# First taps on ScalarE, one parked group, another group order and wider blocks in a convolution plus MLP kernel

## The chip, the cores and the metric

The kernel runs on one core of one Trainium2 chip. The metric is the device time of one execution in microseconds (us); where several executions were timed, the median is given. PE is TensorE, PEld its weight loads, DVE VectorE, ACT ScalarE, POOL GpSimd, SP the engine that issues most DMAs.

## The reference

```python
# x: (8, 4224, 192) f32, weight: (8 heads, 7 taps), w_ch1: (192, 768), w_ch2: (768, 192)
w = softmax(weight, axis=-1)                       # per head
x_pad = six zero rows ahead of each sequence
a[b, s, h, :] = sum_k w[h, k] * x_pad[b, s + k, h, :]     # causal convolution, 24 channels a head
xn = (a - mean(a)) / sqrt(var(a) + 1e-6) * g_ln           # over the 192 channels
out = a + relu(xn @ w_ch1) @ w_ch2
```

## The kernel before

Each of the 128 partitions holds 33 consecutive rows of a sequence. A sequence is worked off in groups of n rows a partition: 16 and 17 for seven sequences, and four smaller groups for the first one, so that TensorE can start early. The mean is folded into the first weights and the factor 1/std is applied at the end, so `up` needs only the transposed convolution. PSUM is the memory that the matmuls write; here it is used as eight banks. To move a finished bank out, so that it can be written again, is called its eviction: ScalarE does it for `up` (L371), VectorE for `down` (L394).

```python
for n in (6, 8, 10, R - 24) if b == 0 else (J - 1, J):   # R = 33, J = 17: 6, 8, 10, 9, then 16, 17
...
xpool: bufs=2   ypool: bufs=3   hid ("ht"): bufs=1   psum: 8 banks of 512 f32, one tag, taken in turn
...
def first_tap(g):                # y = tap 0 * x, one instruction a head (n x 24 elements)
    ...                          # groups 0 and 1 on ACT (L284), all others on DVE (L286)
def conv(g):                     # y += tap k * x shifted by k: 6 taps x 8 heads on DVE (L294)
def transpose(g): ...            # DVE, 32 x 32 blocks (L302)
def stats(g): ...                # DVE: bn_stats a row (L315), then a short chain to 1/std

def up(g):                       # first matmul, four 32-row tiles at a time, into four banks
    half = n if n <= 11 else (n + 1) // 2
    for f in range(NF):                                   # 6 slices of 128 hidden units
        for i0 in range(0, n, half):                      # blocks of rows
            ph = [psum.tile([P, 512], F32, tag="ps", ...) for q in range(NQ)]
            for c in range(NC):                           # 6 channel chunks
                for q in range(NQ):                       # one "round": four matmuls, w columns
                    nc.tensor.matmul(ph[q][:, 0:w], w1[rows, c, fs], t[rows, js, c, :], ...)   # L366
            for q in range(NQ):
                nc.scalar.activation(ht[g][:, f, js, q, :], ph[q]..., AF.Relu)                # L371

def down(g):                     # second matmul, two rows to a bank
    for i0 in range(0, n, 2):
        po = psum.tile([P, 512], F32, tag="ps", ...)
        ... six matmuls a row into po (L389) ...
        for j, dst in zip(js, at):
            nc.vector.scalar_tensor_tensor(out=yg[:, j, :], in0=dst, scalar=rstd..., in1=yg[:, j, :],
                                           op0=ALU.mult, op1=ALU.add)                         # L394
        ... output DMA when a group is done ...

first_tap(0); conv(0); centre_w1(); keep_warm(24); first_tap(1); transpose(0); ... prepare w2 ...
for g in range(NG):
    if g + 2 < NG: load_x(g + 2)
    if g == 0: conv(1)
    up(g)
    if g + 1 < NG:
        if g > 0: first_tap(g + 1); conv(g + 1)
        transpose(g + 1)
    stats(g)
    down(g)
```

Each engine works off its own instructions in program order, and waits by semaphores for data, for a PSUM bank or for a buffer. The float32 matmuls count as two instructions each in the trace.

Of the kernel before, what the change touches and what calls it, by code (L numbers as in the profile page):

```python
# [7 lines left out]
F32 = mybir.dt.float32  # L8
# [3 lines left out]
ALU = mybir.AluOpType  # L12
# [4 lines left out]
def kernel(  # L17
# [23 lines left out]
    nc = tc.nc  # L41
    PSUM = bass.MemoryType.PSUM
    B, S, D = x.shape
    H, K = weight.shape
    F = moe_w_ch1.shape[1]
    P = 128
    Q = 64
    C = 32
    GRP = D // H
    PAD = K - 1  # L50
    R = S // P
    J = 17
    NF = F // P
# [7 lines left out]
    groups = []  # L61
    for b in range(B):
        j0 = 0
        for n in (6, 8, 10, R - 24) if b == 0 else (J - 1, J):
            groups.append((b, j0, n))
            j0 += n
        assert j0 == R
    assert max(n for _, _, n in groups) <= J
    NG = len(groups)
# [4 lines left out]
    outr = out.rearrange("b (p r) d -> b p (r d)", p=P)  # L74

    consts = ctx.enter_context(tc.tile_pool(name="consts", bufs=1))
    setup = ctx.enter_context(tc.tile_pool(name="setup", bufs=1))
# [5 lines left out]
    psum = ctx.enter_context(tc.tile_pool(name="ps", bufs=8, space=PSUM))  # L83
# [54 lines left out]
    for r in range(2):  # L138
        nc.scalar.dma_start(out=gb[Q * r : Q * r + Q, :], in_=g_col[P:D, :])
    nc.sync.dma_start(  # L140
        out=taps, in_=bass.AP(tensor=weight.tensor, offset=0, ap=[[0, P], [K, H], [1, K]])
    )
    nc.sync.dma_start(
        out=raw1[:, 0:2].rearrange("p s f w -> p (s f w)"), in_=w1_words[0:P, :]
    )
    for r in range(2):
        nc.sync.dma_start(
            out=raw1[Q * r : Q * r + Q, 2, :, :].rearrange("p f w -> p (f w)"),
            in_=w1_words[P:D, 2 * FH * r : 2 * FH * (r + 1)],
# [3 lines left out]
        out=raw2.rearrange("p (c d) w -> p c (d w)", d=D),  # L153
        in_=w2_words.rearrange("(c p) d -> p c d", p=P),
# [78 lines left out]
    for q in range(NQ):  # L233
        m = copy[C * q : C * q + C].rearrange("p (q i) -> p q i", q=NQ)
        nc.gpsimd.affine_select(
            out=m, in_=m, pattern=[[0, NQ], [-1, C]],
# [37 lines left out]

    y, yt, rstd = {}, {}, {}

    def first_tap(g):
        n = groups[g][2]
        y[g] = ypool.tile([P, J, D], F32, tag="y", name=f"y{g}")
        for h in range(H):  # L280
            cs = slice(h * GRP, h * GRP + GRP)
            dst, src, tap = y[g][:, 0:n, cs], xg[g][:, 0:n, cs], taps[:, h, 0:1]
            if g < 2:
                nc.scalar.mul(dst, src, tap)  # L284
            else:
                nc.vector.tensor_scalar(out=dst, in0=src, scalar1=tap, scalar2=None, op0=ALU.mult)  # L286

    def conv(g):
        n = groups[g][2]
        t = xg.pop(g)  # L290
        for k in range(1, K):
            for h in range(H):
                cs = slice(h * GRP, h * GRP + GRP)
                nc.vector.scalar_tensor_tensor(  # L294
                    out=y[g][:, 0:n, cs], in0=t[:, k : k + n, cs], scalar=taps[:, h, k : k + 1],
                    in1=y[g][:, 0:n, cs], op0=ALU.mult, op1=ALU.add,
                )

    def transpose(g):
        n = groups[g][2]  # L300
        yt[g] = tpool.tile([P, J, NC, C], F32, tag="yt", name=f"yt{g}")
        nc.vector.transpose(  # L302
            yt[g][:, 0:n].rearrange("p j c t -> p (j c t)"),
            y[g][:, 0:n].rearrange("p j d -> p (j d)"),
        )

    def stats(g):
        n = groups[g][2]
        st = spool.tile([P, J, nc.vector.BN_STATS_DIM], F32, tag="st", name=f"st{g}")
        dt = spool.tile([P, J], F32, tag="d", name=f"d{g}")  # L310
        vt = spool.tile([P, J], F32, tag="v", name=f"v{g}")
        rt = spool.tile([P, J], F32, tag="r", name=f"r{g}")
        d, v, r = dt[:, 0:n], vt[:, 0:n], rt[:, 0:n]
        for j in range(n):
            nc.vector.bn_stats(out=st[:, j, :], in_=y[g][:, j, :])  # L315


        nc.vector.tensor_tensor(d, st[:, 0:n, 1], st[:, 0:n, 4], op=ALU.subtract)
        nc.vector.tensor_tensor(v, st[:, 0:n, 2], st[:, 0:n, 5], op=ALU.add)
        nc.vector.scalar_tensor_tensor(  # L320
            out=d, in0=d, scalar=0.25, in1=d, op0=ALU.mult, op1=ALU.mult
        )
        nc.vector.scalar_tensor_tensor(
            out=v, in0=v, scalar=1.0 / D, in1=d, op0=ALU.mult, op1=ALU.add
        )
        nc.vector.tensor_scalar(v, v, scalar1=1e-6, scalar2=None, op0=ALU.add)


        nc.vector.tensor_single_scalar(
            d.bitcast(U32), v.bitcast(U32), 1, op=ALU.logical_shift_right  # L330
        )
        nc.vector.tensor_scalar(
            out=r.bitcast(I32), in0=d.bitcast(I32), scalar1=-1.0, scalar2=float(0x5F3759DF),
            op0=ALU.mult, op1=ALU.add,
        )
        for _ in range(3):
            nc.vector.tensor_tensor(d, r, r, op=ALU.mult)  # L337
            nc.vector.scalar_tensor_tensor(  # L338
                out=d, in0=d, scalar=-0.5, in1=v, op0=ALU.mult, op1=ALU.mult
            )  # L340
            nc.vector.scalar_tensor_tensor(  # L341
                out=r, in0=d, scalar=1.5, in1=r, op0=ALU.add, op1=ALU.mult
            )
        rstd[g] = rt
# [3 lines left out]
    def up(g):  # L348
        n = groups[g][2]
        t = yt.pop(g)  # L350
        ht[g] = hpool.tile([P, NF, J, NQ, C], F32, tag="ht", name=f"ht{g}")

        half = n if n <= 11 else (n + 1) // 2
        for f in range(NF):
            fs = slice(f * P, f * P + P)
            for i0 in range(0, n, half):
                js = slice(i0, min(i0 + half, n))
                w = (js.stop - js.start) * C
                ph = [
                    psum.tile([P, 512], F32, tag="ps", name=f"ph{g}_{f}_{i0}_{q}")  # L360
                    for q in range(NQ)
                ]
                for c in range(NC):
                    for q in range(NQ):
                        rows = slice(C * q, C * q + C)
                        nc.tensor.matmul(  # L366
                            ph[q][:, 0:w], w1[rows, c, fs], t[rows, js, c, :],
                            start=(c == 0), stop=(c == NC - 1),
                        )
                for q in range(NQ):  # L370
                    nc.scalar.activation(  # L371
                        ht[g][:, f, js, q, :],
                        ph[q][:, 0:w].rearrange("p (j t) -> p j t", t=C), AF.Relu,
                    )

    def down(g):
        b, j0, n = groups[g]
        t = ht.pop(g)
        yg = y.pop(g)

        ends = (n,) if g + 1 < NG else (4, 8, 12, 14, 16, n)
        done = 0
        for i0 in range(0, n, 2):
            js = range(i0, min(i0 + 2, n))
            po = psum.tile([P, 512], F32, tag="ps", name=f"po{g}_{i0}")
            at = [po[:, i * D : i * D + D] for i in range(len(js))]
            for j, dst in zip(js, at):
                for f in range(NF):
                    nc.tensor.matmul(  # L389
                        dst, t[:, f, j, :, :].rearrange("p q t -> p (q t)"), w2[:, f, :],  # L390
                        start=(f == 0), stop=(f == NF - 1),
                    )
            for j, dst in zip(js, at):
                nc.vector.scalar_tensor_tensor(  # L394
                    out=yg[:, j, :], in0=dst, scalar=rstd[g][:, j : j + 1],
                    in1=yg[:, j, :], op0=ALU.mult, op1=ALU.add,
                )
            if js[-1] + 1 in ends:
                end = js[-1] + 1
                nc.sync.dma_start(  # L400
                    out=outr[b, :, (j0 + done) * D : (j0 + end) * D],
                    in_=yg[:, done:end].rearrange("p j d -> p (j d)"),
                )
                done = end


    first_tap(0)
    conv(0)
    centre_w1()
    keep_warm(24)  # L410
    first_tap(1)
    transpose(0)
    words_2 = (
# [4 lines left out]
    for g in range(NG):  # L418
        if g + 2 < NG:
            load_x(g + 2)  # L420
        if g == 0:
            conv(1)
        up(g)
        if g + 1 < NG:
            if g > 0:
                first_tap(g + 1)
                conv(g + 1)
            transpose(g + 1)
        stats(g)
        down(g)  # L430


# [28 lines left out]
```

## Time and profile before

| | before |
|---|---|
| median | 1080.33 us (1079.67 to 1080.75, 5 runs) |
| span of the profiled execution | 1078.5 us |
| busy: PE, DVE, ACT | 98%, 70%, 24% |
| mean granted TensorE clock | 0.997 |

Three groups of instructions, from the list of groups by shape (line, engine, operation, out<-in, shapes, count | busy us, mean ns of one | idle time just before them and what ended it):

```profile
L366 PE MATMUL ph<-yt,w 32*128 32x256 f32 x6336 | 357.7, 377 | 4.3 <-DVE y L394 4.3
L371 ACT ACTIVATE ht<-ph 128x256 f32<-128x256 f32 x528 | 160.0, 390 | 418.3 <-PE ph L366 418.3
L394 DVE SCALAR_TENSOR_TENSOR y<-po,r,y 128x192 f32<-128x192 f32 x264 | 96.8, 412 | 306.2 <-PE po L389 304.3
```

ACT and DVE wait hundreds of microseconds for PE, which costs nothing: PE is the bound. The one figure that costs is the small one, 4.3 us in which PE waited for L394.

### The profile page before, as it was taken

Reading aid. Unit: us, or ns where it says so; the run is one execution under the profiler, and the core shown is the slowest. Engines: PE = TensorE matmul, PEld = TensorE weight load, DVE = VectorE, ACT = ScalarE, POOL = GpSimd, SP = SyncE. Lnnn points to the kernel's source line nnn. Section 1 sums busy time; section 2 is a strip of 40 time slices with the busy share of each in tenths; the row PEclk is TensorE's granted clock in tenths of the full one; section 3 lists DMA queues with packets and bytes.
Section 4 is the critical chain, followed back from the end, with each engine's and each line's share of the span. In section 5 each row is a group of like instructions: output and inputs, shape, how many; then the busy total and the mean of one; then the engine's idle time right before and its main releaser. Section 6 shows DMA issues by size and latency. Waiting matters only on the chain.

```text
span 1078.5 us, 27860 instructions
## 1 busy us (share of the span) xinstructions
PE 1057.6 (98%) x12488; PEld 997.0 (92%) x12488; DVE 753.5 (70%) x1851; ACT 255.4 (24%) x806; POOL 11.1 (1%) x23
## 2 busy tenths in 40 slices
PE   4999999999999999999999999999999999999998
PEld 3988998998999999999999989999899999999998
DVE  7999699849397692957749396693947849297301
ACT  5322122214031230403204041130402214031230
POOL 1000000000000000000000000000000000000000
PEclk9999999999999999999999999999999999999999
DMA  5122123030030300303021030301203030010101
GB/s 184 60 79 111 38 86 115 2 111 35 1 144 1 144 2 16 129 2 144 1 96 50 1 145 1 144 2 51 94 1 144 2 123 23 1 64 1 60 2 63
DMA packets 7718, 66.69 MB, mean 62 GB/s; under 512 B 1199, under 2 KB 2351, under 8 KB 3758
## 3 DMA queue, kind: packets, MB, share of 16 engines
q1 hardware_dynamic: 7294, 64.91, 15.8%
q8 instruction: 97, 1.59, 0.6%
q14 instruction: 23, 0.19, 0.1%
q10 hardware_dynamic: 304, 0.00, 0.0%
HBM read 38.95 MB, written 25.95 MB: 60 GB/s over the span
## 4 chain that ended last, share of the span: by engine, by line
PE 91%; DVE 8%; DMA 1%; issue 0%; ACT 0%; SPq 0%; DVEq 0%
PE ph L366 45%; PE po L389 45%; DVE y L294 5%; DVE yt L302 1%; DMA room<-in_moe_w_ch_dram 1%; DVE st L315 0%; DVE y L286 0%; DVE y L394 0%; ACT room L174 0%; DVE room L182 0%; DVE power L182 0%; DVE w L188 0%; ACT power L174 0%; DVE d L338 0%; DVE r L341 0%
## 5 line engine op out<-in xcount | busy, mean ns | idle before, releaser
L366 PE MATMUL ph<-yt,w 32*128 32x256 f32 (+3 forms) x9216 | 524.0, 383 | 4.3 <-DVE y L394 4.3
L366 PEld LDWEIGHTS ph<-yt,w 32*128 32x128 f32 x9216 | 471.6, 186 | 53.3 <-DVE y L394 5.8
L389 PEld LDWEIGHTS po<-w,ht 128*128 128x128 f32 x3168 | 514.3, 190 | 6.0 <-issue 6.0
L389 PE MATMUL po<-w,ht 128*128 128x192 f32 x3168 | 519.6, 327 | 0.0
L294 DVE SCALAR_TENSOR_TENSOR y<-xg,taps,y 128x384 f32<-128x384 f32 (+5 forms) x864 | 429.8, 578 | 0.0
L371 ACT ACTIVATE ht<-ph 128x256 f32<-128x256 f32 (+3 forms) x768 | 237.8, 396 | 772.3 <-PE ph L366 772.3
L394 DVE SCALAR_TENSOR_TENSOR y<-po,r,y 128x192 f32<-128x192 f32 x264 | 96.8, 412 | 306.2 <-PE po L389 304.3
L315 DVE BATCH_NORM_STATS2 st<-y 128x6 f32<-128x192 f32 x264 | 69.7, 341 | 0.0
L302 DVE STREAM_TRANSPOSE yt<-y 128x3072 f32<-128x3072 f32 (+5 forms) x18 | 56.0, 3112 | 0.6
L286 DVE TENSOR_SCALAR y<-xg,taps 128x408 f32<-128x408 f32 (+3 forms) x128 | 43.1, 410 | 0.0
L106 POOL MEMSET xg<- 1x1152 f32 x7 | 7.3, 1047 | 819.2 <-DMA xg<-in_x_dram 432.2
L244 PE MATMUL pm<-room 128*128 128x384 f32 x4 | 3.1, 880 | 12.3 <-DVE room L190 12.3
L244 PEld LDWEIGHTS pm<-room 128*128 128x128 f32 x4 | 1.2, 324 | 12.9 <-issue 12.9
L337 DVE TENSOR_TENSOR d<-r 128x16 f32<-128x16 f32 (+5 forms) x54 | 9.4, 175 | 1.9
L341 DVE SCALAR_TENSOR_TENSOR r<-d,r 128x16 f32<-128x16 f32 (+5 forms) x54 | 9.4, 175 | 1.9
L338 DVE SCALAR_TENSOR_TENSOR d<-d,v 128x16 f32<-128x16 f32 (+5 forms) x54 | 9.4, 174 | 1.9
L272 PEld LDWEIGHTS idle<-room 128*128 128x128 f32 x48 | 5.4, 192 | 0.5 <-ACT w L266 0.5
L272 PE MATMUL idle<-room 128*128 128x128 f32 x48 | 5.6, 277 | 0.0
L284 ACT ACTIVATE y<-xg,taps 128x144 f32<-128x144 f32 (+1 forms) x16 | 5.5, 473 | 0.0
L266 ACT COPY w<-pw 128x384 f32<-128x384 f32 x12 | 4.7, 546 | 1.4 <-PE pw L261 1.4
L245 PE MATMUL pm<-room 128*128 128x384 f32 x4 | 3.1, 880 | 1.2 <-DVE room L190 1.2
L245 PEld LDWEIGHTS pm<-room 128*128 128x128 f32 x4 | 1.2, 324 | 2.9 <-issue 2.9
(48 smaller groups left out, 59.5 us busy)
## 6 DMA issues: line engine op xcount, KB each, us to landing
xg<-in_x_dram SPq DMA_DIRECT2D x7, 2208.0 KB, 12.3
xg<-in_x_dram SPq DMA_DIRECT2D x7, 2112.0 KB, 11.7
out_dram<-y SPq DMA_DIRECT2D x7, 1536.0 KB, 6.0
out_dram<-y SPq DMA_DIRECT2D x6, 1632.0 KB, 6.5
xg<-in_x_dram SPq DMA_DIRECT2D x1, 1536.0 KB, 6.3
xg<-in_x_dram SPq DMA_DIRECT2D x1, 1440.0 KB, 7.6
xg<-in_x_dram SPq DMA_DIRECT2D x1, 1344.0 KB, 10.6
raw<-in_moe_w_ch_dram SPq DMA_DIRECT2D x1, 1152.0 KB, 7.9
```

What stands on the lines that cost most here:

```text
L272: nc.tensor.matmul(idle[:, 0:P], less, copy, start=True, stop=True)
L286: nc.vector.tensor_scalar(out=dst, in0=src, scalar1=tap, scalar2=None, op0=ALU.mult)
L294: nc.vector.scalar_tensor_tensor(out=y[g][:, 0:n, cs], in0=t[:, k : k + n, cs], scalar=taps[:, h, k : k + 1], in1=y[g][:, 0:n, cs], op0=AL ...
L302: nc.vector.transpose(yt[g][:, 0:n].rearrange("p j c t -> p (j c t)"), y[g][:, 0:n].rearrange("p j d -> p (j d)"),)
L315: nc.vector.bn_stats(out=st[:, j, :], in_=y[g][:, j, :])
L337: nc.vector.tensor_tensor(d, r, r, op=ALU.mult)
L338: nc.vector.scalar_tensor_tensor(out=d, in0=d, scalar=-0.5, in1=v, op0=ALU.mult, op1=ALU.mult)
L341: nc.vector.scalar_tensor_tensor(out=r, in0=d, scalar=1.5, in1=r, op0=ALU.add, op1=ALU.mult)
L366: nc.tensor.matmul(ph[q][:, 0:w], w1[rows, c, fs], t[rows, js, c, :], start=(c == 0), stop=(c == NC - 1),)
L371: nc.scalar.activation(ht[g][:, f, js, q, :], ph[q][:, 0:w].rearrange("p (j t) -> p j t", t=C), AF.Relu,)
L389: nc.tensor.matmul(dst, t[:, f, j, :, :].rearrange("p q t -> p (q t)"), w2[:, f, :], start=(f == 0), stop=(f == NF - 1),)
L394: nc.vector.scalar_tensor_tensor(out=yg[:, j, :], in0=dst, scalar=rstd[g][:, j : j + 1], in1=yg[:, j, :], op0=ALU.mult, op1=ALU.add,)
```

## The change

Its intent is to let PE run without a gap after setup. ScalarE copies ("parks") group 0's second matmul into SBUF, so that group 1 gets its banks without VectorE. First taps go to ScalarE while `down` runs, except group 3's, whose y buffer is still group 0's. The third and fourth group swap sizes. Blocks of `up` are 512 columns wide in groups of 16 rows, but for the last slice.

```diff
-        for n in (6, 8, 10, R - 24) if b == 0 else (J - 1, J):
+        for n in (6, 8, 9, R - 23) if b == 0 else (J - 1, J):
...
-    def first_tap(g):
+    def first_tap(g, on_act=True):
...
-            if g < 2:
+            if on_act:
                 nc.scalar.mul(dst, src, tap)
...
-        half = n if n <= 11 else (n + 1) // 2
         for f in range(NF):
+            half = n if n <= 11 or n * C <= 512 and f < NF - 1 else (n + 1) // 2
...
     # down(g) keeps its matmuls; the VectorE step and the output DMA move to finish(g)
+    def park(g):
+        parked = setup.tile([P, n, D], F32, name=f"parked{g}")
+        for i0 in range(0, n, 2):
+            for j in range(i0, min(i0 + 2, n)):
+                nc.scalar.copy(parked[:, j, :], po[g][j])
+                po[g][j] = parked[:, j, :]
...
     for g in range(NG):
         if g + 2 < NG:
             load_x(g + 2)
-        if g == 0:
-            conv(1)
         up(g)
         if g + 1 < NG:
-            if g > 0:
-                first_tap(g + 1)
-                conv(g + 1)
+            conv(g + 1)
             transpose(g + 1)
-        stats(g)
+        if g != 1:
+            stats(g)
         down(g)
+        if g == 0:
+            park(0)
+        elif g == 1:
+            stats(1)
+            finish(0)
+            finish(1)
+        else:
+            finish(g)
+        if g + 2 < NG:
+            first_tap(g + 2, on_act=g != 1)
```

## The prediction

> **What bounds the kernel now.** I read the page's busy shares first. TensorE is busy for 98% of the span, VectorE 70%, ScalarE 24%, so only time in which TensorE stands still or runs slowly is to be had. Then I read the chain of work that ended last, in order of time (start, length, what):
>
> ```profile
> 53.56 1.55 DVE st L315 x6
> ...
> 58.24 0.75 DVE y L394 x2
> 59.00 0.04 issue
> 59.04 16.20 PE ph L366 x238
> 75.24 15.80 PE po L389 x96
> 91.04 19.59 PE ph L366 x288
> ...
> 168.07 0.32 DVE y L394
> ...
> 168.87 33.03 PE ph L366 x570
> 201.90 31.40 PE po L389 x192
> 233.29 33.21 PE ph L366 x576
> ...
> 1042.00 33.36 PE po L389 x204
> 1075.37 0.03 issue
> 1075.39 0.42 DVE y L394
> ```
>
> L366 is the first matmul, `up`; L389 the second, `down`; L394 the VectorE step that scales a `down` result and adds it to y, and so frees its PSUM bank. From 201.90 to 1075 the chain is TensorE alone. It leaves TensorE only before 30 us (setup), at 53 to 59 us and at 130 to 169 us. At 59 us, group 1's `up` needs a bank in which group 0's `down` result still lies; VectorE was busy with conv(1) until 51.76, then transpose and statistics. At 168 us, group 4's `up` waits in the same way for group 3's result, behind first tap and conv of a group of 16.
>
> The stretches tell what the two places cost: the two disturbed `up` phases of groups 1 and 4, then clean ones of 17 and of 16 rows (columns: bounds, length, busy time by engine, granted TensorE clock, DMA):
>
> ```profile
> 53.98:75.24 21.26, 19.49 (x290) 16.89 (x289) 20.67 (x70) 6.44 (x22) 0.00 (x0) 0.92 0.28 100
> 165.65:201.90 36.25, 33.77 (x578) 31.10 (x577) 35.73 (x78) 13.72 (x46) 1.05 (x1) 0.95 0.23 86
> 233.29:266.50 33.21, 33.21 (x578) 29.42 (x577) 33.13 (x64) 13.97 (x44) 0.00 (x0) 1.00 0.31 118
> 299.85:331.14 31.29, 31.29 (x578) 29.42 (x577) 31.21 (x58) 13.34 (x44) 1.05 (x1) 1.00 0.33 125
> ```
>
> A clean `up` of 16 rows takes 31.29 us; group 4's took 36.25, so 4.96 are lost. Group 1 has 8 rows: half of (31.29 - 0.21) plus 0.21 for the phase's start (worked out below) is 15.75; it took 21.26, so 5.51 are lost. Together 10.5 us, though the list of waits puts only 4.3 us of TensorE idle down to L394. The rest is the last column but two: the clock. In the shorter stretches after each wait it is halved:
>
> ```profile
> 60.00:62.00 2.00, 2.00 (x25) 1.50 (x27) 2.00 (x9) 0.00 (x0) 0.00 (x0) 0.76 0.44 182
> 62.00:64.00 2.00, 2.00 (x24) 1.78 (x20) 2.00 (x7) 0.00 (x0) 0.00 (x0) 0.50 1.05 297
> 64.00:66.00 2.00, 2.00 (x36) 1.85 (x36) 2.00 (x6) 1.21 (x4) 0.00 (x0) 0.88 1.01 403
> ...
> 171.00:173.00 2.00, 2.00 (x24) 1.73 (x23) 2.00 (x7) 0.74 (x3) 0.00 (x0) 0.50 0.54 221
> ```
>
> That is 0.08 x 21.26 + 0.05 x 36.25 = 3.5 us of clock; the other 7 us is waiting, part of it bank by bank.
>
> **What the Trainium skill says.** "TensorE: Matmul & The Clock Gate", Part 1: the clock is gated to half after an idle window of about 3.4 us and released after a busy one. The trace agrees: 0.50 after each wait. The same page, "Back-to-back issue gap": a warm matmul costs N/2.4 + 2.5 ns. The trace agrees: a `down` phase of 17 rows takes 33.35 us and one of 16 takes 31.40, so 12 instructions of 192 columns take 1.95 us, 162.5 ns each = 2 x 192/2.4 + 2.5 (an fp32 matmul is two instructions, each two cycles a column). "ScalarE: Activation LUTs", "What ACT_TABLE_LOAD costs": 186 ns + 0.833 ns an element, about 93 more for a pointer operand, 93 overlapped. The trace agrees: eight first taps of 192 elements take 2.96 us, 347 ns apart by the formula. "PSUM — Partial Sum Buffer", on bank collisions: engines must be kept apart by bank. In the trace L394 comes in pairs, 3.9 us apart, after both rows of a bank; parking copies will come in pairs too.
>
> **The change part by part.**
>
> 1. *Parking group 0.* ScalarE copies each bank into SBUF as it is filled; group 1 then needs no VectorE. Evictions of 192 columns at L371 take 1.00 us for four, so a copy about 0.25. Group 0's `down` ends at 54.06; the last pair is out at about 54.7. Counting tiles around the eight banks (15 in setup, 24 for group 0's `up`, 3 for `down`), group 1's first block takes banks 2 to 5 and its second 6, 7, 0, 1; `down` used 7, 0, 1. The second block starts one block of 12 rounds x 216 ns = 2.6 us after 53.98, at 56.6. Parked in time by 1.9 us: the 5.5 us go.
>
> 2. *First taps on ScalarE.* VectorE loses 8 instructions a group, 43.1 us in all at L286 less the eight of one group that stay (about 2 us). ScalarE gains 8 x (280 + 0.833N - 93): 3.1 us for 9 rows (N = 216), 4.1 to 4.2 for 16 and 17. It lies within `down` of 31 us, when ScalarE has nothing to do, so the 41 us are worth nothing as such. What counts is group 4: its conv starts straight after group 2's finish, not 2.7 us later.
>
> 3. *Groups 9, 10 for 10, 9.* TensorE's sum stays. The phase pair under which VectorE does conv(4) of 16 rows becomes 10 rows long: 3.9 us longer. Following VectorE with the durations of the trace: stats(0) ends 58.2; conv(2) of 9 rows 17.1, transpose 1.9, stats(1) 5.3, finish(0) 2.0, finish(1) 2.7: 87.2. First tap(3) waits for group 0's output (issued about 84.6, 3.1 us): 87.8, ends 89.9. conv(3) of 10 rows 18.4, transpose 2.1, stats(2) 5.6: 116; finish(2) follows TensorE to 121.5. conv(4) 25.4, transpose 3.4, stats(3) 5.8: 156.1. TensorE without waits: group 1 from 53.98 with 15.75 + 15.80, group 2 (9 rows) 17.67 + 17.75 from 85.5, group 3 (10 rows) 19.59 + 19.71 from 120.9, so group 4 at 160.3. VectorE is done with stats(3) 4.2 us before; before the change stats(3) ended at 168, 2.4 us after group 4 began. Only the last pair of L394 is then open, ready at 161.1, and its bank is needed with the second block, at 165.4. The 5.0 us go.
>
> 4. *Blocks of 512 columns.* Seven groups have 16 rows; in five of six slices two blocks of 256 become one. Excess of a phase over its columns: 0.39 us with 72 rounds (19.59 for 10 rows against 72 x 266.7 ns), 0.57 with 144 (31.29 against 144 x 213.3): 2.5 ns a round and 0.21 a phase. Sixty rounds fewer: 0.15 us a group, 1.05 in all. Evicting 4 x 512 columns takes 3 x 0.49 + 0.6 = 2.1 us against 2.6 of the shortest block beside it: hidden.
>
> Sum: 1080.3 - 5.5 - 5.0 - 1.05 = **1068.8 us**, 1.1% less. Setup to 29.9 us and the last 3 us are untouched.
>
> **Rivals.**
>
> *A new wait replaces the old.* Two slacks are thin. ScalarE is in order: first tap(2) sits between parking and group 1's first eviction, 54.7 to about 57.7. That eviction (1.21 us) is done at 58.9; the third block wants its banks at 59.2. And finish(1) at 87.2 has 1.3 us before group 2's second block at 88.5. A short miss costs tenths; one of over 2 us halves the clock again and costs 3 to 5: 1072 to 1074. For it: the slacks. Against: each term is a duration of the trace, and a wait in group 1 delays TensorE's need too.
>
> *ScalarE or VectorE becomes the bound.* ScalarE goes to about 255 + 60 = 315 us; the first taps stand outside `up`, where evictions are urgent. VectorE falls to about 712. Neither can be it; the time would stay at 1069. A first tap blocked by a late load or by y's buffer would hold ScalarE up, but loads land 12.3 us after an issue at the start of `up`, and the first tap comes 31 us after.
>
> *The waits go, the time doesn't*: if the clock dropped anyway, only 7 of the 10.5 us come back: 1072. Against: every later stretch that I read has 1.00.
>
> *The 512 blocks cost or give more.* If the 2.5 ns were per phase instead, 1069.8; if all 0.57 us of excess were per round, 0.24 us a group, 1068.2.
>
> **Range and chances.** Centre 1068.8. Below, little is left: 1067.3 would need the larger gain from blocks and shorter phase starts. Above, one thin slack missed: 1072. Over 2% faster needs 1058.7, ten below what removing all waiting gives: 1%. Slower by 2% would need a steady wait in each group: 1%.
>
> **What would show it.** TensorE's idle before L366 put down to L394 should fall from 4.3 us to under 0.5 and the clock be 1.00 in all stretches of two us between 54 and 66 and between 160 and 180; group 4's `up` should start at about 160; clean `up` phases of 16 rows should take 31.14 us. A wait of L366 on ScalarE near 59, or on L394 near 88, would make me wrong, as would a time at or above 1074.

## The result and the profile after

| | before | after |
|---|---|---|
| median | 1080.33 us | 1069.61 us (1069.35 to 1070.14, 5 runs) |
| ratio after / before | | 0.9903 (95%: 0.9888 to 0.9917) |
| span of the profiled execution | 1078.5 us | 1068.3 us |
| busy: PE, PEld, DVE, ACT (us) | 1057.6, 997.0, 753.5, 255.4 | 1049.9, 907.0, 714.3, 304.7 |

A ratio is the mean time of one kernel's runs over that of the other's in the same rounds, so it is not quite the ratio of the medians. The whole interval lies below 1, so the 1% is real.

The chain that ended last, after the change (start us, length us, what). In this kernel L367 is `up`, L389 `down`, L410 the VectorE step, L400 the parking copy, L372 the eviction of `up`, L284 a first tap on ScalarE:

```profile
31.08 12.24 PE ph L367 x287
43.33 11.90 PE po L389 x72
55.23 15.75 PE ph L367 x288
...
141.79 19.70 PE po L389 x120
161.49 31.14 PE ph L367 x336
192.63 31.40 PE po L389 x192
...
1031.84 33.36 PE po L389 x204
```

From 31.08 us to the end the chain does not leave TensorE. Group 1's `up` takes 15.75 us where it took 21.26, and group 4's takes 31.14 where it took 36.25. The stretches after the two former waits (columns: bounds, length, then busy time and instructions of PE, PEld, DVE, ACT, POOL, then granted clock, DMA share, GB/s):

```profile
55.23:70.98 15.75, 15.75 (x289) 14.66 (x289) 15.27 (x55) 9.39 (x30) 0.00 (x0) 1.00 0.20 84
62.00:64.00 2.00, 2.00 (x44) 1.90 (x40) 2.00 (x7) 0.77 (x3) 0.00 (x0) 1.00 0.03 8
...
161.49:192.63 31.14, 31.14 (x337) 17.12 (x337) 31.07 (x52) 11.54 (x24) 1.05 (x1) 1.00 0.27 103
```

The clock is 1.00 in each, where 62 to 64 us had 0.50 before. Two thin places that the prediction named can be read from the timeline (start, length, engine, line, operation, operands, count): ScalarE around group 1's start, and VectorE around group 4's.

```profile
55.26 0.54 ACT L400 COPY parked<-po 128x192 f32<-128x192 f32 x2 [3.36 <-PE po L389]
55.69 3.03 ACT L284 ACTIVATE y<-xg,taps 128x216 f32<-128x216 f32 x8
58.63 1.18 ACT L372 ACTIVATE ht<-ph 128x256 f32<-128x256 f32 x4
...
157.23 2.69 DVE L410 SCALAR_TENSOR_TENSOR y<-po,r,y 128x192 f32<-128x192 f32 x8
161.53 0.74 DVE L410 SCALAR_TENSOR_TENSOR y<-po,r,y 128x192 f32<-128x192 f32 x2 [1.60 <-PE po L389]
```

Group 1's first eviction ends at 59.8 us; its third block wants the banks two blocks and a phase start after 55.23, at 60.6. VectorE is through with four of group 3's five banks at 159.9, before group 4's `up` starts at 161.5.

From the list of groups by shape: the new form of 512 columns and the first taps of 408 elements on ScalarE.

```profile
L367 PE MATMUL ph<-yt,w 32*128 32x512 f32 x1680 | 182.2, 589 | 0.0
L372 ACT ACTIVATE ht<-ph 128x512 f32<-128x512 f32 x140 | 72.3, 602 | 305.8 <-PE ph L367 305.8
L284 ACT ACTIVATE y<-xg,taps 128x408 f32<-128x408 f32 x56 | 30.2, 643 | 0.0
```

ScalarE gained 49 us of work and PE never waits for it.

A measure that is cleaner than the whole time is the stretch from the first matmul of group 0's `down` to the end of the last matmul. It leaves out the loads and setup. It is 1033.27 us in the profile of before and 1021.94 in that of after: 11.33 us less. The medians fell by 10.7 only, so some 0.6 us were given back outside the stretch; that is taken up below. (The profiled run of before is its median, 1080.33; that of after is the slowest of its five, 1070.14, so in the two profiles 1.1 us were given back.)

### The profile page after: what moved, and what is told of

It reads as the page before. It is cut to its first block, busy times and chain, and to the rows that moved or that the text cites. A ratio compares the mean times of both kernels' runs of the same rounds, so it can differ in the third digit from the quotient of the medians.

```text
span 1068.3 us, 24401 instructions
## 1 busy us (share of the span) xinstructions
PE 1049.9 (98%) x10808; PEld 907.0 (85%) x10808; DVE 714.3 (67%) x1731; ACT 304.7 (29%) x792; POOL 11.1 (1%) x23
## 4 chain that ended last, share of the span: by engine, by line
PE 97%; DVE 2%; DMA 1%; issue 0%; ACT 0%; DVEq 0%
PE po L389 49%; PE ph L367 48%; DVE y L294 1%; DMA xg<-in_x_dram 1%; DMA ga<-in_moe_g_ln_dram 0%; DVE yt L302 0%; ACT room L174 0%; DVE room L182 0%; DVE y L410 0%; DVE room L171 0%; DVE room L165 0%; DVE room L167 0%; DVE room L190 0%; DVEq L294 0%
## 5 line engine op out<-in xcount | busy, mean ns | idle before, releaser
L389 PE MATMUL po<-w,ht 128*128 128x192 f32 x3168 | 519.6, 327 | 0.0
L389 PEld LDWEIGHTS po<-w,ht 128*128 128x128 f32 x3168 | 514.3, 190 | 6.0 <-issue 6.0
L367 PE MATMUL ph<-yt,w 32*128 32x256 f32 (+4 forms) x7536 | 516.9, 431 | 0.7 <-DVE yt L302 0.7
L367 PEld LDWEIGHTS ph<-yt,w 32*128 32x128 f32 x7536 | 381.8, 185 | 132.5 <-issue 98.6
L372 ACT ACTIVATE ht<-ph 128x256 f32<-128x256 f32 (+4 forms) x628 | 225.2, 444 | 701.7 <-PE ph L367 701.7
L410 DVE SCALAR_TENSOR_TENSOR y<-po,r,y 128x192 f32<-128x192 f32 x258 | 95.4, 412 | 332.9 <-PE po L389 331.8
L284 ACT ACTIVATE y<-xg,taps 128x384 f32<-128x384 f32 (+4 forms) x136 | 67.8, 605 | 0.0
L400 ACT COPY parked<-po 128x192 f32<-128x192 f32 x6 | 1.6, 322 | 10.1 <-PE po L389 10.1
L318 DVE TENSOR_TENSOR d<-st 128x16 f32<-128x16 f32 (+5 forms) x18 | 3.3, 185 | 0.6
```

What stands on the lines that cost most here:

```text
L284: nc.scalar.mul(dst, src, tap)
L372: nc.scalar.activation(ht[g][:, f, js, q, :], ph[q][:, 0:w].rearrange("p (j t) -> p j t", t=C), AF.Relu,)
L389: nc.tensor.matmul(dst, t[:, f, j, :, :].rearrange("p q t -> p (q t)"), w2[:, f, :], start=(f == 0), stop=(f == NF - 1),)
L410: nc.vector.scalar_tensor_tensor(out=yg[:, j, :], in0=src, scalar=rstd[g][:, j : j + 1], in1=yg[:, j, :], op0=ALU.mult, op1=ALU.add,)
```

## The experiments

All ran with five rounds against the kernel before. "Stretch" is the measure just described, from each run's own profile; the stretch of the changed kernel is 1021.94 us in all three profiles of it.

| run | what | median us | ratio to before | stretch us | against after |
|---|---|---|---|---|---|
| e1_no_park | group 0 not parked | 1075.26 | 0.9959 | 1027.37 | +5.43 |
| e2_taps_on_dve | first taps on VectorE | 1070.55 | 0.9912 | 1022.38 | +0.44 |
| e3_order_10_9 | old group order | 1070.48 | 0.9910 | 1022.48 | +0.54 |
| e4_taps_and_order | both of these | 1074.59 | 0.9953 | 1026.59 | +4.65 |
| e5_blocks_256 | old blocks | 1070.51 | 0.9910 | 1022.98 | +1.04 |
| e6_blocks_512_all | 512 in the last slice too | 1074.24 | 0.9944 | 1025.78 | +3.84 |
| r5, r6 | the changed kernel again | 1070.20, 1069.59 | 0.9908, 0.9905 | 1021.94 both | 0 |
| e7_before_warm | before, PE busy in its waits | 1077.31 | 0.9973 | 1029.91 | |
| b2_before_again | before again | 1080.75 | 1.0006 | 1031.60 | |
| i1_pool_conv | after, part of conv(0) on GpSimd | 1073.09 | 0.9939 | 1021.94 | 0 |
| i2_nine_adds | the same, smaller | 1071.22 | 0.9920 | 1021.94 | 0 |

### Parking undone (e1_no_park)

```diff
         if g == 0:
-            park(0)
+            finish(0)
         elif g == 1:
             stats(1)
-            finish(0)
             finish(1)
```

> The changed kernel with group 0's second matmul finished by VectorE from PSUM (as before the change), all else kept. Theory (TensorE's wait for group 0's banks was the loss at 53 to 59 us, and TensorE has no slack later to win it back): the first up of 8 rows grows from 15.75 to about 21 us, with a wait of L367 on VectorE and a clock near 0.5 for some 4 us after it; the time is 5.0 to 5.5 us longer than the changed kernel, 1074.6 to 1075.2 us. Rival (parking is worth little, the group order and the first taps carry the gain): within 1 us of 1069.6 us.

Measured: 1075.26 us, the stretch 5.43 us longer. The chain and a two-microsecond stretch of this run:

```profile
59.92 16.20 PE ph L367 x238
```

```profile
62.00:64.00 2.00, 2.00 (x28) 1.77 (x24) 2.00 (x7) 0.00 (x0) 0.00 (x0) 0.56 1.24 393
```

The wait is back, with the same 16.20 us piece for the last 238 instructions as before the change, and the clock falls to 0.56 after it. Nothing later wins it back. The theory holds; the rival, that parking is worth little, falls. The 5.43 hold such a fall of the clock; the mean granted clock is 0.996 to 0.998 in all five timed runs of e1, and 1.000 in those of the changed kernel.

### First taps, group order, and both (e2, e3, e4)

```diff
-            first_tap(g + 2, on_act=g != 1)     # e2, e4
+            first_tap(g + 2, on_act=False)
...
-        for n in (6, 8, 9, R - 23) if b == 0 else (J - 1, J):     # e3, e4
+        for n in (6, 8, 10, R - 24) if b == 0 else (J - 1, J):
```

> The changed kernel with the first taps of groups 2 to 17 on VectorE, all else kept. Theory (VectorE's 41 us lie beside TensorE's work and only the slack at groups 2 and 4 counts): finish(1) ends 2.1 us later, at about 90.1 against a need at 89.6 for the last banks, so 0.5 to 0.9 us are lost at group 2; at group 4 a slack of about 4 us shrinks to 1.5 us and nothing is lost. 1069.9 to 1070.6 us. Rival (freeing VectorE is what shortened the kernel): several us longer, 1073 us or more.

> The changed kernel with groups 6, 8, 10, 9 as before the change. Theory: stats(3) ends at about 161.2 us, TensorE wants a bank of group 3 at 161.5 and gets it at 162.0: about 0.5 us lost, too short for the clock to drop; 1069.9 to 1070.4 us. Rival (the order is what cures group 4): the wait of about 3 us comes back with its clock drop, 1073.5 to 1075 us.

> Both undone: first taps of groups 2 to 17 on VectorE and groups 6, 8, 10, 9; parking and blocks of 512 kept. Theory (the two are two cures for one wait, each enough alone): 1.7 us lost at group 2 and 3 us of wait plus 1.8 us of halved clock at group 4, 1075 to 1078 us, far more than the sum of the two single runs' losses (about 1.4 us). Rival (the parts add): about 1071 us.

Measured: +0.44 us, +0.54 us, and +4.65 us together. In e2 the chain has 18.11 us for group 2's `up` in place of 17.67 and a clean 31.14 for group 4's, so its loss lies at group 2. In e3 it has 31.69 for group 4's `up` in place of 31.14, and a clean 19.59 for group 2's. From the chains of e2 and of e3:

```profile
86.76 18.11 PE ph L367 x288
```

```profile
161.32 31.69 PE ph L367 x335
```

Each is lost where the theory put it. Together they cost almost five times the sum of the two. In the chain of e4:

```profile
86.39 21.06 PE ph L367 x288
...
165.70 31.19 PE ph L367 x328
```

Group 2's `up` takes 21.06 us where a clean one of 10 rows takes 19.59, so 1.47 are lost there. Group 4's `up` starts at 162.5 us, stops after a few instructions until 165.70, and loses the other 3.2 us. So at group 4 the two parts are two cures for one wait, and each leaves about half a microsecond or less alone. At group 2 it is similar on a smaller scale: 0.44 us for the taps, nothing for the order, 1.47 for both. That is not what "freeing 41 us of VectorE" would suggest: with the new order kept, moving those 41 us back costs 0.44 us.

One part of the expectation missed: 1074.59 us lies below its 1075 to 1078. The clock stayed at 1.00 in all stretches of e4's profile after its wait, so the 1.8 us put down for a halved clock did not come there. It came in some executions: the mean granted clock is 1.000 in the three of e4 that took 1073.92 to 1074.59 us, 0.998 in the two that took 1075.66 and 1075.91, which lie in the range. The runs of the kernel before, below, vary in the same way.

### Blocks of 256 and of 512 columns (e5, e6)

```diff
-            half = n if n <= 11 or n * C <= 512 and f < NF - 1 else (n + 1) // 2
+            half = n if n <= 11 else (n + 1) // 2      # e5
+            half = n if n * C <= 512 else (n + 1) // 2      # e6
```

> The changed kernel with blocks of 256 columns in the groups of 16 rows, as before the change. Theory (2.5 ns a round of four matmuls, 60 rounds more in each of seven groups): clean up phases of 16 rows 31.29 us instead of 31.14, time 1.05 us longer, 1070.6 us. Rivals: overhead by phase alone, no difference, 1069.6 us; all the excess by round, 1.7 us longer, 1071.3 us.

> The changed kernel with blocks of 512 columns in the last slice too. Theory (the first row of down needs the last slice's four evictions, which end 2.2 us after its matmuls, while the ten instructions for the other five slices last 1.6 us plus 0.2 us of switching): a wait of about 0.4 us of TensorE on ScalarE in each of seven groups, 2 to 3 us longer, 1071.6 to 1072.6 us. Rival (the eviction is hidden): 0.2 us shorter, 1069.4 us.

Measured in e5: the stretch is 1.04 us longer and a clean `up` of 16 rows takes 31.29 us, as predicted. The whole time moved from 1070.20 us in the run of the changed kernel beside it to 1070.51, which is less, since the setups of the two profiles differ by 0.67 us the other way; the stretch is the reading to trust.

Measured in e6: 1074.24 us, the stretch 3.84 us longer, or 0.55 a group where 0.4 was expected. The timeline at the start of group 4's `down`:

```profile
192.63 1.89 PE L389 MATMUL po<-w,ht 128*128 128x192 f32 x10
192.72 2.06 ACT L372 ACTIVATE ht<-ph 128x512 f32<-128x512 f32 x4 [3.08 <-PE ph L367]
...
194.83 5.47 PE L389 MATMUL po<-w,ht 128*128 128x192 f32 x32 [0.31 <-ACT ht L372]
```

TensorE does the ten instructions of the first row's other five slices, then waits until the four evictions are done at 194.78. Ten at 162.5 ns would have ended their issue at 194.26; the next starts at 194.83. This is why the change keeps narrow blocks in the last slice, and it also shows that a wait of half a microsecond costs half a microsecond and no clock.

### The clock after a wait (e7_before_warm, b2_before_again)

In the kernel before, idle matmuls were put ahead of the block that waits. They write into a bank that the block's first real matmul overwrites, so the result stays right.

```diff
+                for _ in range({(1, 1, 0): 10, (4, 0, 0): 12}.get((g, f, i0), 0)):
+                    nc.tensor.matmul(
+                        ph[0][:, 0:P], w2flat[:, 0:P], w2flat[:, 0:P], start=True, stop=True
+                    )
                 for c in range(NC):
```

> The kernel before, with 10 and 12 idle matmuls of 128 columns on TensorE (2.2 and 2.6 us, into a bank that the next real matmul overwrites) in the two places where it waits for VectorE, at groups 1 and 4. The waits stay, TensorE is busy in them. Theory (of the 10.5 us lost, 3.5 are the halved clock after the waits): the clock stays at 1.00 and 3 to 3.5 us come back, 1076.8 to 1077.3 us. Rival (the low clock costs nothing beside the waits): 1080.3 us.

> The kernel before, unaltered, to see when its setup ends. In two profiles of that kernel and its variant the second matmul of group 0 began at 42.2 and 42.3 us; in eight profiles of the changed kernel and its variants at 42.9 to 43.7, about 1 us later, and the chain there starts with later landings of the first loads. If the difference belongs to the kernel: again 42.0 to 42.4 us. If it is scatter of the first transfers from run to run: 42.5 to 43.7 us. The time should agree with its own reference within 0.1%, about 1080.3 us.

Measured in e7: 1077.31 us, the stretch 3.36 us shorter than in the first profile of before. L364 is the idle work; chain, then a stretch:

```profile
57.00 2.43 PE ph L364 x20
...
164.21 2.68 PE ph L364 x24
```

```profile
62.00:64.00 2.00, 2.00 (x44) 1.90 (x40) 2.00 (x7) 1.04 (x4) 0.00 (x0) 1.00 1.10 315
```

The waits stay, and TensorE does useless work in them; the clock stays at 1.00, and 3 us come back. So of the 11.33 us between the two stretches about 3.4 are the halved clock, some 7 are waiting, and 1.04 the blocks. This holds for the first profile of before, in which the clock fell at both places.

b2, the unaltered kernel, tells more than it was run for. Its stretch is 1.67 us shorter than in the first profile of the same kernel. The same two microseconds of the first profile and of b2:

```profile
170.00:172.00 2.00, 2.00 (x30) 1.76 (x28) 2.00 (x7) 0.00 (x0) 0.00 (x0) 0.57 0.06 24
```

```profile
170.00:172.00 2.00, 2.00 (x44) 1.90 (x40) 2.00 (x8) 0.33 (x2) 0.00 (x0) 1.00 0.01 4
```

After the same wait at group 4 the clock fell in one execution and not in the other. So the gain in the stretch is 11.33 us against the one and 9.66 against the other. The timed runs vary with it: 1078.64 to 1081.71 us for the kernel before, but 1069.35 to 1070.45 for the changed kernel, whose TensorE never waits after setup, and 1077.11 to 1077.34 for e7, whose clock is 1.000 in all five. Of the 26 runs of before beside the experiments, the nine with a mean clock of 0.998, as in b2's profile with one fall, took 1078.64 to 1080.19 us; the seventeen with 0.996 or 0.997, as in the first profile with two falls, took 1079.94 to 1081.71. So the clock makes a good part of the spread; that it makes all of it was not shown.

### The setup (r5_after_again, r6_after_third)

> The changed kernel itself, unaltered, as the reference for the runs beside it and to see whether its setup, in which conv(0) began 1.17 us later than in the profile of before, repeats. If the late start belongs to the change: conv(0) again at about 16.0 us. If it is scatter of the first transfers: another value, between 14.8 and 16.5 us. Time 1069.4 to 1070.1 us.

> The changed kernel, unaltered, as the reference for the run beside it on the same chip: 1069.4 to 1070.3 us. Its second matmul of group 0 begins at 42.9 to 43.7 us if the later setup belongs to the kernel; near 42.2 us if it is scatter.

| profile | conv(0) starts | group 0's `down` starts |
|---|---|---|
| before, b2, e7 (a variant of before) | 14.87, 15.12, 15.00 us | 42.09, 42.34, 42.23 us |
| after, r5, r6 | 16.04, 16.37, 15.63 us | 43.26, 43.59, 42.85 us |
| e1 to e6 | 15.53 to 16.14 us | 42.87 to 43.36 us |
| i2, i1 | 15.85, 14.97 us | setup altered |

The instructions of setup are the same and in the same order in before and after, yet in the changed kernel the first loads land later: the taps are first read at 5.64 us instead of 4.90, the first weights at 8.66 instead of 7.49. It repeats in r5 and r6 and in the six variants e1 to e6, and not in i1, also a variant, whose conv(0) starts at 14.97. By the start of `down` it is 1.0 us, on the mean of the three profiles in each of the first two rows. Both readings that were set against each other thus have a run against them, and the cause stays open.

### Two tries at a faster version (i1_pool_conv, i2_nine_adds)

After the change only setup is left to win, and its longest piece is conv(0) on VectorE, 13.5 us.

```diff
# i1: heads 6 and 7 of conv(0); i2: only (tap 1-3, head 6) and (tap 1-6, head 7)
+                prods[k, h] = setup.tile([P, n, GRP], F32, name=f"prod{k}_{h}")
+                nc.scalar.mul(prods[k, h], xg[0][:, k : k + n, cs], taps[:, h, k : k + 1])
...
+                nc.gpsimd.tensor_tensor(
+                    y[0][:, 0:n, cs], y[0][:, 0:n, cs], prods[k, h], op=ALU.add
+                )
...
-    keep_warm(24)
+    keep_warm(4)        # i1; 20 in i2
```

> The changed kernel with two of the eight heads of group 0's conv taken off VectorE: ScalarE makes their twelve products, GpSimd adds them (12 adds of 144 elements), 4 idle matmuls in setup instead of 24. Theory (after the change only the setup ahead of TensorE's first up is left to win, and conv(0) on VectorE is its longest piece): conv(0) shrinks from 13.5 to about 10.1 us, the first up starts near 27.7 us instead of 31.1, all later waits stay away since VectorE and TensorE both come earlier: 1066 to 1067 us. Rivals: GpSimd's adds or ScalarE's delayed copies of the centred weights set the start (first up at 29 to 30 us, 1068 to 1069 us); or VectorE slows beside GpSimd and nothing is won.

> The changed kernel with nine of conv(0)'s 48 steps off VectorE (head 6, taps 1 to 3, and head 7, taps 1 to 6: products on ScalarE, adds on GpSimd at the 1.14 us each that the run before showed) and 20 idle matmuls in setup, so that TensorE has no idle stretch before the first up. Theory: nine adds end 10.3 us after the first product, conv(0) on VectorE shrinks from 13.5 to 11.0 us, both end together; the first up starts 2.4 us earlier than in the changed kernel of the same chip at an equal start of conv(0), and its clock is 1.00: 1067 to 1068 us, 2 to 2.5 us less than the changed kernel beside it. Rival (GpSimd's adds become the wait again, or VectorE runs slower beside them): 0 to 1 us won.

Measured: 1073.09 and 1071.22 us, against 1070.20 and 1069.59 of the changed kernel. The timeline of i1:

```profile
14.97 10.13 DVE L315 SCALAR_TENSOR_TENSOR y<-xg,taps,y 128x144 f32<-128x144 f32 x36
16.64 13.73 POOL L305 TENSOR_TENSOR y<-y,prod 128x144 f32<-128x144 f32 x12 [11.83 <-ACT prod L298]
```

VectorE was quicker by the 3.4 us expected, but GpSimd needs 13.73 us for 12 adds, so its adds became the wait, as the first rival had it: the transpose stood until 30.40. That is not 1.14 us for each add, as the expectation of i2 read it. The timeline of GpSimd alone in two windows, 16.5 to 25.4 us and from 25.46 us:

```profile
16.64 8.81 POOL L305 TENSOR_TENSOR y<-y,prod 128x144 f32<-128x144 f32 x1 [11.83 <-ACT prod L298]
```

```profile
25.41 4.95 POOL L305 TENSOR_TENSOR y<-y,prod 128x144 f32<-128x144 f32 x11
```

The first add alone lasted 8.81 us. It ended at 25.45, just after VectorE's unbroken run of conv steps (14.97 to 25.10); the other eleven, beside an idle VectorE, came 0.45 us apart. TensorE had idled 6.8 us by then, since the idle matmuls had been cut, and group 0's `up` took 14.04 us instead of 12.24 at a clock of 0.50 in its first four microseconds. In i2 the adds were sized to 1.14 us each, and the same thing came again. From its timelines of VectorE and of GpSimd:

```profile
15.85 6.79 DVE L318 SCALAR_TENSOR_TENSOR y<-xg,taps,y 128x144 f32<-128x144 f32 x24
24.17 5.95 DVE L318 SCALAR_TENSOR_TENSOR y<-xg,taps,y 128x144 f32<-128x144 f32 x15 [1.54 <-POOL y L303]
```

```profile
17.52 5.47 POOL L303 TENSOR_TENSOR y<-y,prod 128x144 f32<-128x144 f32 x1 [12.71 <-ACT prod L297]
```

GpSimd's first add did not end until 22.99 us, just after VectorE had stopped at 22.64 to wait for a handed-over sum. Of VectorE's last 15 steps, the six beside the remaining adds then came some 0.57 us apart, as did those adds, and the nine after them 0.28 again. So both halves of i2's rival came true, GpSimd's adds were the wait and VectorE ran slower beside them; 1.6 us were lost, where it put 0 to 1 us won. In both runs the first add ended 0.35 us after VectorE stopped, whether that took 8.81 or 5.47 us, so a fixed cost of a first add does not explain it; no run had the adds alone from the start. Neither beats the changed kernel, which stays the fastest that ran.

## Why the prediction was right, point by point

- **The bound and the loss.** TensorE's work is the time, and the loss sat in two `up` phases. Shown: after the change the chain is TensorE alone from 31.08 us to the last matmul, and the stretch is the same 1021.94 us in five profiles, among them i1 and i2, whose setup differs.
- **Step 1, parking, 5.5 us.** Right: 5.43 by e1, and 15.75 us for group 1's `up`, the very figure worked out.
- **Steps 2 and 3, first taps and order, 5.0 us.** The size is right for the profile of before that was read: what is left of the 11.33 us after parking and blocks is 4.86. It was not sure to come: 1.8 of the 5.0 were the halved clock at group 4, and against b2, where the clock did not fall there, 3.19 are left. The sharing was told one-sidedly. The text said that what counts of the first taps is group 4; e2 shows that with the new order they count only at group 2, with 0.44 us, and e3 and e4 show that order and first taps stand in for each other at group 4. One sum is off without consequence: 8 x (280 + 0.833N - 93) gives 2.9 us for 9 rows, not 3.1; the trace has 3.03.
- **Step 4, blocks, 1.05 us.** Right: 1.04 by e5, and 31.14 us a phase.
- **The thin slacks.** At group 1's third block 0.3 us was predicted and about 0.8 found; at group 2's second block 1.3 was predicted, and the profile has finish(1) done at 88.04, against a need at 89.6 (12 rounds of 242.5 ns after 86.71). At group 4 VectorE's stats(3) end 4.2 us ahead of TensorE, as worked out. Neither short miss came.
- **The clock, 3.5 us.** Right in kind: e7 gives 3.36. The prediction took the drop as sure to follow a wait of over 2 us, and read it as agreeing with an idle window of 3.4 us, though the waits were 1.77 and 2.48 us. The profiles show no such mark: the clock fell after 1.77 us at group 1 in before, b2 (1.78) and e1, and did not after 2.06 us in e4 or 2.48 us at group 4 in b2.
- **Setup untouched.** Here is most of the small miss of 0.8 us, 1068.8 against 1069.61. TensorE's part fell by 11.33 us against 11.55 predicted, which makes 0.2; the remaining 0.6 is the time outside the stretch. In the profiles setup came out about 1 us later, by loads that landed later; what made them later stays open. No term of the sum covered it.

## What to carry to other kernels

Where one engine is the bound, compare the length of each phase with that of an undisturbed one of the same shape: here two phases lost 10.5 us while the list of waits showed 4.3. Two measures that each win some 4 us against a wait may be one measure done twice, and only a run with both undone shows it. A mean over several instructions can hide that one of them stood still: twelve adds in 13.73 us were one of 8.81 and eleven of 0.45. Work taken off an engine that isn't the bound is worth the slack that it makes at one wait, not its own 41 us.

## What the Trainium skill lacked or had wrong

- The Trainium skill's page "TensorE: Matmul & The Clock Gate", Part 1, speaks of an idle window of about 3.4 us. Here TensorE idled 1.77 us (group 1) and 2.48 us (group 4) in the trace's records, and the clock fell to 0.50 for some 3.4 us (the lost clock of the stretches from 60 to 66 us, 1.7 us, over one half), beginning 1.4 to 2.3 us after work had resumed (before, b2, e1). The same wait at group 4 dropped the clock in one profile of the kernel before and not in the other, and a wait of 2.06 us in e4 did not. The page calls the window free-running, which fits; that one wait shorter than the window can cost 1.7 us of clock, or none, it doesn't say.
- The same page gives about 2.5 ns for each matmul, and "TensorEngine Tiling (Array Packing)", Instruction Overhead, about 60 cycles, told there for narrow matmuls. Neither gives it for a stream of rounds of four row tiles. With four 32-row tiles, 60 rounds of four instructions fewer a group saved 0.15 us, so it is 2.5 ns for a round, not for each of its four.
- "GPSIMD Engine Reference", section 3.1 (Elementwise), gives about 2.6 cycles an element for a two-input add (312 ns for 144 elements at 1.2 GHz) and names the dispatch without a figure. In i1 the eleven adds of 144 elements that ran without VectorE came 0.45 us apart, so the dispatch would be some 0.13 us of each, an estimate from the page's figure and that spacing.
- No page has the later landing of the first loads, 4.90 against 5.64 us for the taps, between two kernels with the same setup; the runs leave its cause open.
